# Issuing the first 25 slots of a top-k attention and MLP kernel step by step from a table

## The chip, the core and the metric

The kernel runs on one core of one Trainium2 chip. The core has a matrix engine (TensorE, PE in the profile, with its weight loads shown as PEld), a vector engine (VectorE, DVE), a scalar engine (ScalarE, ACT), a general engine (GpSimd, POOL) and an engine that only issues transfers (SyncE, SP). Each engine works through its own queue in order; between engines, an instruction waits on semaphores. The metric is the device time of one execution in microseconds.

## The reference

```python
# q, k, v: (8 batches, 8 heads, 576 positions, 64)
scores = q @ k.T / sqrt(64)                       # per batch and head, 576 x 576
kth = 32nd largest score of each row
scores = where(scores >= kth, scores, -1e9)
attn = softmax(scores)                            # sum + 1e-9 in the denominator
x = (attn @ v) -> (4608 tokens, 512)              # heads side by side
h = x @ w_in                                      # 512 -> 2048
g = h * sigmoid(1.702 * h)
out = g @ w_out                                   # 2048 -> 512
```

All data is float32.

## The kernel before, in words

**Slots.** The attention is cut into 144 slots, 18 per batch. A slot holds 128 rows of two heads. For a slot, TensorE computes the scores (`scores`, L339) into one pair of PSUM banks that all slots share; ScalarE copies them to SBUF (`copy_scores`, L350); VectorE pairs the two halves of each row by maximum and minimum (`pair_up`, L360), which frees the banks for the next scores; and VectorE then finds the 32 largest in four rounds of MAX8 and three of MATCH_REPLACE8 (`topk`, L386 and L390). GpSimd makes the threshold and the shift of the exponent from the result (`bounds`, L404 and L405). One slot later ScalarE masks (`mask`, L418) and exponentiates (`exps`, L428), which also gives the row sums `den`. `invert` adds 1e-9 (L437 on GpSimd for n > 11, L439 on VectorE up to slot 11) and takes the reciprocal on VectorE (L441).

**From probabilities to x.** Up to slot 10 the probabilities are turned on TensorE against a diagonal of the reciprocals, which GpSimd makes (`divide`, L448; `turn`, L468 and L471), and ScalarE copies the result out (L476). From slot 11 GpSimd scales them (`normalize`, L454), ScalarE splits them into halves (`split`, L490), SP writes them to DRAM (`rows<-sc`, L492) and reads them back transposed (`pt<-rows`, L498). TensorE multiplies with v (`values`, L526; `values_at`, L557; `values_of_two`, L586) and ScalarE copies the result into x.

**The MLP.** When 128 rows of x are whole they form a block. A block is worked off in four units: `hidden` (TensorE, L662), `tanh` (ScalarE, L678), `gate`, `combine` and `project` (TensorE, L760 for the first two blocks, L776 for the others). `tanh(False)` leaves the hidden values in PSUM, and then `gate` is one VectorE instruction (L693). `tanh(True)` copies them to SBUF too (L681), and then `gate` is two GpSimd instructions (L690, L691).

**The weights.** w_in and w_out come in 32 pieces, loaded by SP (L134) and rounded in steps: size (ScalarE or GpSimd), shift (VectorE, L158), low (ScalarE, L159), sign and addition (GpSimd, L148 and L151). Two or three pieces belong to each of the slots 0 to 10.

**What sets the order.** The order is written by hand and taken as it stands, with no scheduler: `opening`, then `slot(n)` for slots 0 to 10, `filling` for 11 to 20, then `steady_pair(n)` for two slots at a time from 21 on, to the last slot. Within these functions the calls issue their instructions at once; an engine's queue holds them in the order of the calls. `stay_warm` (L174) issues matmuls of the identity whose result is not used. TensorE's pieces have three tile sizes: 128x128 (the first two blocks' MLP, the turning), 128x64 (the other blocks' MLP, the values) and 64x64 (scores, ends of the values).

The lines that the change touches stand in `invert`, `slot`, `filling_slot` and at the end of the kernel:

```python
    with tc.manual_schedule():
        opening()
        for n in range(SETTLED + 1):
            slot(n)
        filling()
        for n in range(STEADY + 8, N + 2, 2):
            steady_pair(n)
```

Of the kernel before, what the change touches and what calls it, by code (L numbers as in the profile page):

```python
# [9 lines left out]
ALU = mybir.AluOpType  # L10
# [19 lines left out]
TO_ZERO = 2.0**-100  # L30


@with_exitstack
def kernel(
    ctx: ExitStack,
# [23 lines left out]

    nc = tc.nc

    B, H, S, D = q.shape
    C = H * D
# [23 lines left out]
    PAIRED = SETTLED + 1  # L89
    STEADY = PAIRED + 2  # L90
# [25 lines left out]
    both_banks = [ps_p.tile([P, 512], F32, name=f"po{i}") for i in range(2)]  # L116

    ident = const.tile([P, P], F32, name="ident")
    make_identity(nc, ident[:])
    win = const.tile([P, CC, DFF], F32, name="win")  # L120
    wout = const.tile([P, FC, C], F32, name="wout")

# [47 lines left out]
    def stay_warm(count, of=ident[:]):  # L170

        none = both_banks[1][:]
        for i in range(count):
            nc.tensor.matmul(none[:, 0:P], lhsT=of, rhs=of, start=True, stop=True)  # L174
# [147 lines left out]
    N = len(slots)  # L322
# [110 lines left out]
    def invert(n):  # L433

        some = small.tile([P, 2], F32, name="some", tag="sums")
        if n > PAIRED:
            nc.gpsimd.tensor_scalar(some[:], st[n]["den"][:], 1e-9, None, op0=ALU.add)  # L437
        else:
            nc.vector.tensor_scalar_add(some[:], st[n]["den"][:], 1e-9)  # L439
        rden = st[n]["rden"] = small.tile([P, 2], F32, name="rden", tag="inverse")  # L440
        nc.vector.reciprocal(rden[:], some[:])  # L441

# [190 lines left out]
    class Block:  # L633
        def __init__(self, place, rows):
            self.place, self.rows = place, rows
            self.whole = len(blocks_seen) < WHOLE
            self.bank = 1 - len(blocks_seen) % 2
            blocks_seen.append(self)
            self.left = list(range(FC))
            if not self.whole:  # L640
                self.left = [h * (FC // 2) + 2 * u + c for u in range(4) for h in range(2) for c in range(2)]
            self.done = 0
# [30 lines left out]
    def tanh(aside):  # L673

        if to_gate:
            ph, fs, x = to_gate.pop(0)
            th = thp.tile([P, G * P], F32, name="th")
            nc.scalar.activation(th[:], ph, AF.Tanh, scale=0.851 / RAISE)  # L678
            if aside:
                h = thp.tile([P, G * P], F32, name="h", tag="th")  # L680
                nc.scalar.copy(out=h[:], in_=ph)  # L681
                ph = h[:]
            gated.append((th, ph, fs, x, aside))
# [223 lines left out]
    def opening():  # L907

        stay_warm(8, v_tail[:, 0, :, :].rearrange("p j d -> p (j d)"))
        load("q", 0, 0, nc.sync)  # L910
        load("k", 0, 0, nc.scalar)
        for hp in range(2):
            for name in "qk":
                if hp:
                    load(name, 0, hp)
        for x in by_slot[0]:
            load_piece(x)
        prepare_first()
        scores(0)
        pair_first()  # L920
        stay_warm(2)
        for name in "qk":
            prepare_main(name, 0, 1)
        stay_warm(8)
        prepare_ends(0, 1)
        early.extend(round_piece(x) for x in by_slot[0])
        for piece in early:
            piece["size"]()
        scores(1)
        copy_scores(1)  # L930
        prepare_rest()
        for hp in range(2, NP):
            for name in "qk":
                load(name, 0, hp)
        load_v(0, 0)
        for x in by_slot[1]:
            load_piece(x)
# [11 lines left out]
    def slot(n):  # L949

        todo = later.pop(n, [])
        for fn, args in todo:
            if fn not in (prepare, prepare_by_dma, load_piece):
                fn(*args)
        preparing = [(fn, args) for fn, args in todo if fn is prepare or fn is prepare_by_dma]
        some = [round_piece(x) for x in by_slot.get(n, [])] if n else early
        steps = {name: [piece[name] for piece in some] for name in ("size", "shift", "low")}
        last = some[-1] if len(some) > 2 else None
        if last:
            steps["size"].pop()  # L960

        def do(name, count):
            for _ in range(min(count, len(steps[name]))):
                steps[name].pop(0)()

        if n == 0:
            steps["size"].clear()
            do("low", 3)
        else:
            exponentials(n - 1, bring_all if n % 4 == 1 and n > TURNS + 1 else lambda: None)  # L970
            if n == TURNS + 1:
                stay_warm(14)
                bring_all()
            copy_scores(n + 1)
            bring_all()
            if 1 < n <= TURNS:
                turn_main(n - 2)
                turn_ends(n - 2)
            if n > TURNS + 1:
                tanh(False)  # L980
            do("size", 3)
            if n == TURNS + 1:
                do("low", 3)
                tanh(False)
        for i, op in enumerate(topk(n)):
            op()
            if i == 1:
                for _ in range(min(3, len(unfinished))):
                    finish_one()
                if last and n > 2:  # L990
                    last["pool_size"]()
            if i == (9 if n < 3 else 7):
                if n > 0:
                    divide(n - 1)
                if last and n < 3:
                    last["pool_size"]()
                while unfinished:
                    finish_one()
                for fn, args in todo:
                    if fn is load_piece:  # L1000
                        fn(*args)
            if i == 9:
                pair_up(n + 1)
            if i == 12:
                do("shift", 3)
            if i == (13 if n == TURNS + 1 else 10):
                gate()
        bounds(n)
        for piece in some:
            unfinished.extend(piece["finish"][piece is last :])  # L1010
        if n < NP:
            for fn, args in preparing:
                fn(*args)
        if n >= TURNS:
            turn_main(n - 1)
            turn_ends(n - 1)
        do("low", 3)
        if last:
            last["sign"]()
        scores(n + 2)  # L1020
        if n == SETTLED:
            copy_scores(n + 2)
        if n == 0:
            return
        idle = not ready and n < TURNS
        if 1 < n <= TURNS:
            values(n - 2, put_off if n == TURNS else None)
        if n >= TURNS:
            values(n - 1, put_off)
        if n >= NP:  # L1030
            for fn, args in preparing:
                fn(*args)
        if n > PROJECTS and may_project(2):
            project(n == SETTLED)
        if idle:
            stay_warm(8)
        if n == SETTLED:
            turn_qk(1, 0)
        hidden()
# [59 lines left out]
    def filling_slot(n, beside, pool_ahead, behind, pool_behind, late=[]):  # L1099

        todo = later.pop(n, [])
        due = [(fn, args) for fn, args in todo if fn is prepare_by_dma]
        exponentials(n - 1)
        for fn in beside:
            fn()
        for fn in pool_ahead:
            fn()
        find(n, 8)
        for fn, args in todo:
            if fn is load_v:  # L1110
                fn(*args)
        scores(n + 2)
        if n == PAIRED:
            normalize(n - 1)
            split(n - 1)
            copy_scores(n + 2)
        else:
            copy_scores(n + 2)
            normalize(n - 1)
            split(n - 1)  # L1120
        write_all()
        for fn, args in todo:
            if fn not in (prepare_by_dma, load_v):
                fn(*args)
        turn_by_dma(n - 1)
        while turns:
            turns.pop(0)()
        for fn in pool_behind:
            fn()
        bounds(n)  # L1130
        for fn in behind + late:
            fn()
        for fn, args in due:
            fn(*args)
# [106 lines left out]
    def last_units():  # L1241
# [7 lines left out]
        project_one()  # L1249
        leave_all()  # L1250

    with tc.manual_schedule():
        opening()
        for n in range(SETTLED + 1):
            slot(n)
        filling()
        for n in range(STEADY + 8, N + 2, 2):
            steady_pair(n)
        combine()
        while ready or to_gate or gated or to_combine or to_project:  # L1260
            last_units()
        merge_some(len(merging), nc.vector)
        write_all()
# [30 lines left out]
```

## Time and profile before

| what | us |
| --- | --- |
| median of 3 runs (lowest to highest) | 1378.75 (1377.12 to 1379.25) |
| the profiled execution | 1379.59 |
| its span, first to last instruction | 1377.8 |
| busy in the span: PE / DVE / ACT / POOL | 1341.2 / 1286.0 / 1164.1 / 964.4 |

The span is what the profile's rows are counted in, from its start. Two neighbouring records of an engine can overlap, so the mean duration of a record is a little more than what it adds. A busy TensorE is not TensorE at its peak, since matmuls are pipelined and their ends are modelled; a float32 matmul shows as two records.

### The profile page before, as it was taken

The numbers are of one execution on the slowest core, as the hardware profiler recorded it, in microseconds if no ns is written. First come the engines' busy times: TensorE is split into PE (matmuls) and PEld (weight loads), VectorE is DVE, ScalarE is ACT, GpSimd is POOL, SyncE is SP. The second block draws the span as 40 slices with busy tenths as digits, with TensorE's granted clock in tenths as the row PEclk, the third lists the DMA queues.
The fourth block names the chain that finished last, engine by engine and source line by source line (L and its number), as shares of the span: only waits on it lengthen the run. The fifth ranks groups of instructions, "written<-read, shape, count | busy, mean of one in ns | idle before, by whom it ended". The sixth has DMA issues, their size and how long they took to land.

```text
span 1377.8 us, 54398 instructions
## 1 busy us (share of the span) xinstructions
PE 1341.2 (97%) x22560; PEld 1205.0 (87%) x22560; DVE 1286.0 (93%) x3392; ACT 1164.1 (84%) x1930; POOL 964.4 (70%) x1758
## 2 busy tenths in 40 slices
PE   7789999999999999999999999999999999999998
PEld 5676578899999999999999999999998999999998
DVE  7999998999999999999999999999999999999912
ACT  6988887998889888988898988888888998888841
POOL 3776676777777776777777777677777777777770
PEclk8999999999999999999999999999999999999999
DMA  7551568787889786977898668988888768855640
GB/s 232 155 163 62 151 159 198 179 196 196 205 210 211 178 189 173 232 193 192 192 227 208 182 174 193 210 198 191 197 211 208 195 176 183 184 142 135 151 118 17
DMA packets 527223, 246.92 MB, mean 179 GB/s; under 512 B 458880, under 2 KB 505472, under 8 KB 526976
## 3 DMA queue, kind: packets, MB, share of 16 engines
q1 hardware_dynamic: 526544, 243.16, 71.5%
q8 instruction: 177, 2.90, 0.9%
q14 instruction: 70, 0.57, 0.1%
q10 hardware_dynamic: 432, 0.30, 0.1%
HBM read 46.01 MB, written 103.42 MB: 108 GB/s over the span
## 4 chain that ended last, share of the span: by engine, by line
PE 79%; DMA 3%; ACT 1%; issue 0%; POOL 0%; SPq 0%; DVE 0%; DVEq 0%; ACTq 0%; POOLq 0%
PE ph L662 32%; PE po L776 28%; PE o L586 10%; PE s_ps L339 9%; DMA pt<-rows 2%; DMA rows<-sc 1%; ACT pr L428 0%; ACT sc L418 0%; ACT sc L490 0%; ACT sc L350 0%; ACT halves L268 0%; ACT raws L794 0%; SPq L221 0%; POOL pr L454 0%; ACT h L681 0%
## 5 line engine op out<-in xcount | busy, mean ns | idle before, releaser
L386 DVE MAX8 top<-ranked 128x8 f32<-128x288 f32 (+1 forms) x1152 | 637.6, 596 | 0.0
L662 PE MATMUL ph<-xT,win 128*64 128x128 f32 (+1 forms) x8544 | 493.8, 273 | 0.0
L662 PEld LDWEIGHTS ph<-xT,win 128*64 128x64 f32 (+1 forms) x8544 | 469.4, 137 | 27.6 <-issue 24.1
L390 DVE MATCH_REPLACE8 ranked<-top,ranked 128x288 f32<-128x288 f32 (+1 forms) x864 | 462.4, 543 | 0.0
L490 ACT COPY sc<-pr 128x2304 uint16<-128x2304 uint16 x134 | 283.4, 2115 | 90.1 <-POOL pr L454 90.0
L454 POOL TENSOR_SCALAR pr<-pr,rden 128x576 f32<-128x576 f32 x268 | 197.9, 748 | 49.2 <-DVE rden L441 47.7
L428 ACT ACTIVATE pr<-sc,low 128x576 f32<-128x576 f32 x288 | 219.9, 769 | 0.0
L418 ACT ACTIVATE sc<-sc,cut 128x576 f32<-128x576 f32 x288 | 208.6, 779 | 4.7 <-POOL cut L404 4.7
L360 DVE TENSOR_TENSOR ranked<-s_ps,sc 128x576 f32<-128x576 f32 x286 | 201.8, 747 | 3.8 <-ACT sc L350 3.8
L776 PE MATMUL po<-raws,h 128*64 128x128 f32 x2112 | 205.3, 273 | 0.0
L776 PE MATMUL po<-wout,h 128*64 128x128 f32 x2112 | 205.3, 273 | 0.0
L350 ACT COPY sc<-s_ps 128x576 f32<-128x576 f32 x286 | 168.5, 642 | 26.9 <-PE s_ps L339 14.4
L437 POOL TENSOR_SCALAR some<-den 128x2 f32<-128x2 f32 x132 | 29.3, 222 | 221.6 <-ACT pr L428 221.4
L339 PE MATMUL s_ps<-qk_t 64*64 64x288 f32 x2304 | 177.6, 421 | 5.6 <-DVE ranked L360 4.4
L691 POOL TENSOR_TENSOR th<-th,h 128x512 f32<-128x512 f32 x134 | 171.8, 1282 | 11.2
L776 PE MATMUL po<-wout,th 128*64 128x128 f32 x2176 | 165.3, 273 | 0.0
L776 PEld LDWEIGHTS po<-raws,h 128*64 128x64 f32 x2112 | 133.8, 137 | 0.0
L776 PEld LDWEIGHTS po<-wout,h 128*64 128x64 f32 x2112 | 133.7, 137 | 0.0
L776 PEld LDWEIGHTS po<-wout,th 128*64 128x64 f32 x2176 | 127.8, 137 | 0.9 <-POOL wout L739 0.4
L339 PEld LDWEIGHTS s_ps<-qk_t 64*64 64x64 f32 x2304 | 76.2, 134 | 58.1 <-issue 14.8
L586 PE MATMUL o<-pt,v_l 128*64 128x128 f32 (+1 forms) x2240 | 124.8, 265 | 0.0
L586 PEld LDWEIGHTS o<-pt,v_l 128*64 128x64 f32 x2240 | 110.3, 137 | 10.1 <-issue 9.5
(118 smaller groups left out, 1647.5 us busy)
## 6 DMA issues: line engine op xcount, KB each, us to landing
rows<-sc SPq DMA_DIRECT2D x134, 576.0 KB, 4.0
qk_rows<-halves SPq DMA_DIRECT2D x24, 576.0 KB, 5.5
out_dram<-raws SPq DMA_DIRECT2D x68, 128.0 KB, 3.7
raws<-in_moe_w_in_dram SPq DMA_DIRECT2D x16, 512.0 KB, 5.1
raws<-in_moe_w_out_dram SPq DMA_DIRECT2D x16, 512.0 KB, 3.7
qk_l<-in_q_dram SPq DMA_DIRECT2D x28, 256.0 KB, 4.4
qk_l<-in_k_dram SPq DMA_DIRECT2D x28, 256.0 KB, 4.2
v_l<-in_v_dram SPq DMA_DIRECT2D x4, 1024.0 KB, 8.8
```

Source lines behind the costliest of these rows:

```text
L339: nc.tensor.matmul(ps[rows, i, c, 0:HALF], lhsT=qT[b, hps[p]][on, cols], rhs=kT[b, hps[p]][on, FIRST[i] + c * HALF : FIRST[i] + (c + 1) * ...
L360: nc.vector.tensor_tensor(out=ranked[n][:, :, c, :], in0=a, in1=b, op=op)
L386: nc.vector.max(top[:, i, 8 * r : 8 * r + 8], of(r, i))
L390: nc.vector.match_replace(to, top[:, i, 8 * r : 8 * r + 8], of(r, i), LOWEST)
L418: nc.scalar.activation(sc[:, i, :], sc[:, i, :], AF.Prelu, bias=cut[:, i : i + 1], scale=SCALE, alpha=HUGE)
L428: nc.scalar.activation(pr[:, i * S : (i + 1) * S], sc[:, i, :], AF.Exp, bias=low[:, i : i + 1], accum_out=den[:, i : i + 1],)
L454: nc.gpsimd.tensor_scalar(pr[:, i, :], pr[:, i, :], st[n]["rden"][:, i : i + 1], 1.0, op0=ALU.mult, op1=ALU.mult)
L490: nc.scalar.copy(out=halves, in_=pr[:].bitcast(U16).rearrange("p (k h) -> p h k", h=2))
L586: nc.tensor.matmul(o[s][j * D : (j + 1) * D, cols], lhsT=lhsT, rhs=rhs, start=(s, j) not in halves[:k], stop=(s, j) not in halves[k + 1 :],)
L662: nc.tensor.matmul(ph[rows, i * P : (i + 1) * P], lhsT=win[:, c, f * P + rows.start : f * P + rows.stop], rhs=xs[:, x.place, c, :], start= ...
L691: nc.gpsimd.tensor_tensor(out=th[:], in0=th[:], in1=h, op=ALU.mult)
L776: nc.tensor.matmul(both_banks[bank][y * TAIL : (y + 1) * TAIL, to * P : (to + 1) * P], lhsT=a[:, i, :], rhs=weight(w, fs[i])[:, y, :], sta ...
```

## The change

Every engine call of `opening`, `slot`, `filling` and the pairs 21 to 24 is now collected as a step in place of being issued, 2595 steps in all. Then the steps are issued in an order that a table gives, and from slot 25 on everything is issued at once as before. The table moves steps within and between slots, on all five engines; no engine's work is taken out by it. In the built kernel the runs of one tile size on TensorE, up to the end of the table, number 92, where they were 84.

Beside the table: the addition of 1e-9 is on GpSimd for all slots (12 instructions moved from VectorE); the first six gates, those of `slot(5)` to `slot(10)`, go by `tanh(True)`, so six VectorE instructions become six copies on ScalarE and twelve instructions on GpSimd; 14 warming matmuls in slot 5 are left out; the loads of v in `filling_slot` are issued with the other loads, behind the scores. In the built order SP issues the row write that stood just behind batch 1's load of v ahead of that load.

```diff
+COLLECTED = 25
+
+ORDER = """
+8 11 0+8 9 12 10 13+5 22 18 23+2 33 25+2 19 27+5 34 32 20 38+4 35 21 36 97 37 42+4 98 46+4 99 50 54+6 100 53 51
...
+2528+2 2516+2 2530+4 2518+6 2534+2 2585+2
+"""
+
+class Engine:
+    def __init__(self, engines, engine):
+        self.engines, self.engine = engines, engine
+
+    def __getattr__(self, name):
+        do = getattr(self.engine, name)
+
+        def step(*args, **kwargs):
+            if self.engines.collected is None:
+                do(*args, **kwargs)
+            else:
+                self.engines.collected.append(lambda: do(*args, **kwargs))
+
+        return step
+
+class Engines:
+    def __init__(self, nc):
+        self.collected = None
+        for name in ("tensor", "vector", "scalar", "gpsimd", "sync"):
+            setattr(self, name, Engine(self, getattr(nc, name)))
...
-    nc = tc.nc
+    nc = Engines(tc.nc)
...
-        if n > PAIRED:
-            nc.gpsimd.tensor_scalar(some[:], st[n]["den"][:], 1e-9, None, op0=ALU.add)
-        else:
-            nc.vector.tensor_scalar_add(some[:], st[n]["den"][:], 1e-9)
+        nc.gpsimd.tensor_scalar(some[:], st[n]["den"][:], 1e-9, None, op0=ALU.add)
...
             if n == TURNS + 1:
-                stay_warm(14)
+                pass
                 bring_all()
...
             if n > TURNS + 1:
-                tanh(False)
+                tanh(True)
             do("size", 3)
             if n == TURNS + 1:
                 do("low", 3)
-                tanh(False)
+                tanh(True)
...
-        for fn, args in todo:
-            if fn is load_v:
-                fn(*args)
         scores(n + 2)
...
-            if fn not in (prepare_by_dma, load_v):
+            if fn is not prepare_by_dma:
                 fn(*args)
...
+    def issue_in_order():
+
+        steps, nc.collected = nc.collected, None
+        order = list(range(len(steps)))
+        if ORDER.split():
+            order = []
+            for part in ORDER.split():
+                first, _, count = part.partition("+")
+                order += range(int(first), int(first) + int(count or 1))
+        assert sorted(order) == list(range(len(steps)))
+        for i in order:
+            steps[i]()
...
     with tc.manual_schedule():
+        nc.collected = []
         opening()
         for n in range(SETTLED + 1):
             slot(n)
         filling()
-        for n in range(STEADY + 8, N + 2, 2):
+        for n in range(STEADY + 8, COLLECTED, 2):
+            steady_pair(n)
+        issue_in_order()
+        for n in range(COLLECTED, N + 2, 2):
             steady_pair(n)
```

More of the change, by code (lines that the diff above doesn't have):

```diff
@@ L118 @@
     ident = const.tile([P, P], F32, name="ident")
-    make_identity(nc, ident[:])
+    make_identity(tc.nc, ident[:])
     win = const.tile([P, CC, DFF], F32, name="win")
```

81 rows, old and new, of the table ORDER are left out of this document.

## The prediction

> **What bounds the kernel now.** I read the page first (busy shares, clock, chain), then the busy time by stretch, then the waits of the first 262 us, and last the order of single instructions there.
>
> ```profile
> span 1377.8 us, 54398 instructions
> PE 1341.2 (97%) x22560; PEld 1205.0 (87%) x22560; DVE 1286.0 (93%) x3392; ACT 1164.1 (84%) x1930; POOL 964.4 (70%) x1758
> ...
> PEclk8999999999999999999999999999999999999999
> ...
> PE 79%; DMA 3%; ACT 1%; issue 0%; POOL 0%; SPq 0%; DVE 0%; DVEq 0%; ACTq 0%; POOLq 0%
> ```
>
> The chain is TensorE's, but it covers only the last 84% of the span; what comes before shows in the stretches. Their columns are length, then busy time (and instructions) of PE, PEld, DVE, ACT, POOL, then clock, DMA share, GB/s.
>
> ```profile
> core 0: us, PE busy (x) PEld busy (x) DVE busy (x) ACT busy (x) POOL busy (x), PEclk, DMA share, GB/s
> ...
> 10.40:60.00 49.60, 35.97 (x288) 26.86 (x288) 48.59 (x126) 42.99 (x88) 31.34 (x39) 0.83 0.66 208
> 60.00:140.00 80.00, 72.47 (x667) 57.98 (x666) 76.19 (x196) 69.05 (x132) 55.74 (x68) 0.98 0.37 114
> 140.00:220.00 80.00, 74.26 (x923) 55.16 (x923) 77.33 (x207) 69.85 (x119) 58.82 (x90) 1.00 0.68 169
> 220.00:262.20 42.20, 40.77 (x764) 36.74 (x762) 38.12 (x100) 32.36 (x52) 28.87 (x53) 1.00 0.76 185
> 262.20:1300.00 1037.80, 1036.56 (x18550) 949.41 (x18548) 1021.63 (x2706) 921.26 (x1494) 753.57 (x1442) 1.00 0.79 191
> ```
>
> Slots 0 to 24 of VectorE's search run from 10.4 to 262.2 us. From 262.2 on TensorE is busy for 1036.56 of 1037.80 us and the chain is its own. The code of that stage and its order are unchanged, so a microsecond won or lost before 262.2 should appear whole at the end. Before 262.2 VectorE leads: it idles 251.8 − (48.59 + 76.19 + 77.33 + 38.12) = 11.6 us, TensorE 28.3 us, of which 14.7 after 60 us. So the question is how much VectorE time the first 25 slots lose or gain, and whether TensorE keeps up.
>
> **The change part by part.** First what VectorE loses in one old slot (timeline of VectorE; start, duration):
>
> ```profile
> 104.92 0.68 DVE L693 SCALAR_TENSOR_TENSOR th<-th,po 128x512 f32<-128x512 f32 x1
> ...
> 112.40 1.14 DVE L439 TENSOR_SCALAR some<-den 128x2 f32<-128x2 f32 x1 [0.59 <-ACT pr L428]
> 113.57 0.17 DVE L441 RECIPROCAL rden<-some 128x2 f32<-128x2 f32 x1
> 113.65 1.40 DVE L386 MAX8 top<-ranked 128x8 f32<-128x576 f32 x2
> ...
> 117.01 0.68 DVE L693 SCALAR_TENSOR_TENSOR th<-th,po 128x512 f32<-128x512 f32 x1
> ```
>
> The addition waits in VectorE's queue until ScalarE's exponentials are done, and the search waits behind it. The groups up to 262.2 us (count | busy, mean ns | idle before), with GpSimd's addition from the whole run:
>
> ```profile
> L691 POOL TENSOR_TENSOR th<-th,h 128x512 f32<-128x512 f32 x11 | 14.1, 1282 | 0.9
> ...
> L439 DVE TENSOR_SCALAR some<-den 128x2 f32<-128x2 f32 x12 | 7.0, 582 | 4.2 <-ACT pr L428 4.2
> L690 POOL TENSOR_SCALAR th<-th 128x512 f32<-128x512 f32 x11 | 6.8, 621 | 0.0
> ...
> L681 ACT COPY h<-ph 128x512 f32<-128x512 f32 x8 | 4.7, 592 | 0.0
> ...
> L693 DVE SCALAR_TENSOR_TENSOR th<-th,po 128x512 f32<-128x512 f32 x6 | 4.1, 676 | 0.0
> ```
>
> ```profile
> L437 POOL TENSOR_SCALAR some<-den 128x2 f32<-128x2 f32 x132 | 29.3, 222 | 221.6 <-ACT pr L428 221.4
> ```
>
> *Twelve additions (slots 0 to 11) leave VectorE:* 7.0 busy + 4.2 idle, less 0.1 us each because records overlap (113.57 + 0.17 ends after 113.65): 10.0 us off VectorE. GpSimd takes 12 × 0.222 = 2.7 us, and now it does the waiting. VectorE's reciprocal still waits for it, but in the new order it stands later among the search steps. What is queued behind the waiting addition on GpSimd are rounding pieces; GpSimd is busy 55.74 of 80 us between 60 and 140.
>
> *Six gates leave VectorE:* 4.1 less 6 × 0.1 = 3.5 us. GpSimd takes 6 × (0.621 + 1.282) = 11.4 us and ScalarE six more copies, 6 × 0.592 = 3.6 us. Kept at the old three rounding pieces a slot, GpSimd would need about 55.74/80 × 12.1 + 1.9 + 0.2 = 10.5 us in a slot of 117.01 − 104.92 = 12.1 us: not late against the old slot, but against the unloaded 8.63 of below. The new order therefore matters: VectorE's shift of the last six pieces, in slots 9 and 10 before, stands in slots 12 and 13.
>
> *DMA queue.* In the old order SP issues the 1 MB load of batch 1's v and its two tails ahead of a row write:
>
> ```profile
> 217.75 1.41 DVE L360 TENSOR_TENSOR ranked<-s_ps,sc 128x576 f32<-128x576 f32 x2
> ...
> 226.38 1.42 DVE L360 TENSOR_TENSOR ranked<-s_ps,sc 128x576 f32<-128x576 f32 x2
> ...
> 226.58 0.59 SPq L210 DMA_DIRECT2D v_l<-in_v_dram  x1
> ...
> 227.22 1.49 SPq L221 DMA_DIRECT2D v_e<-in_v_dram  x2
> ...
> 228.76 1.14 SPq L492 DMA_DIRECT2D rows<-sc  x1
> ...
> 237.00 1.18 ACT L350 COPY sc<-s_ps 128x576 f32<-128x576 f32 x2 [4.63 <-DMA rows<-sc]
> ...
> 238.22 1.42 DVE L360 TENSOR_TENSOR ranked<-s_ps,sc 128x576 f32<-128x576 f32 x2 [2.99 <-ACT sc L350]
> ...
> 241.37 0.17 DVE L441 RECIPROCAL rden<-some 128x2 f32<-128x2 f32 x1 [1.07 <-POOL some L437]
> ```
>
> The unstalled slot is 226.38 − 217.75 = 8.63 us; the next takes 11.84, and 1.07 more are lost at the reciprocal: 4.3 us, because the write shares the engines with the load. The built order of the changed kernel has this row write ahead of the load on SP. What is late next is the transposing read behind the load, which feeds TensorE two slots later; I count the 4.3 us as won.
>
> VectorE's other idle time, 11.6 − 4.2 − 2.99 − 1.07 = 3.3 us, I leave as it is. Sum on VectorE: 10.0 + 3.5 + 4.3 = 17.8 us.
>
> *TensorE.* Its price and its waits:
>
> ```profile
> 63.69 3.39 PE L174 MATMUL po<-ident 128*128 128x128 f32 x28
> 66.92 3.74 PE L662 MATMUL po<-xT,win 128*128 128x128 f32 x32
> ...
> 102.56 2.88 PE L468 MATMUL tp<-by,pr 128*128 128x128 f32 x16 [2.17 <-POOL by L448]
> ...
> 115.94 1.95 PE L468 MATMUL tp<-by,pr 128*128 128x128 f32 x16
> ...
> 600.53 0.39 PE L776 MATMUL po<-raws,th 128*64 128x128 f32 x4
> 600.75 0.39 PE L776 MATMUL po<-raws,h 128*64 128x128 f32 x4
> ...
> 601.84 3.66 PE L662 MATMUL ph<-xT,win 128*64 128x128 f32 x64
> 605.44 1.20 PE L339 MATMUL s_ps<-qk_t 64*64 64x288 f32 x16
> ```
>
> ```profile
> PE tp L468 <- POOL by L448: 7.0, 4, 3.5
> ...
> PE tp L471 <- ACT pt L476: 6.0, 5, 3.2
> ```
>
> The 14 warming matmuls of slot 5 (28 records) go: 66.92 − 63.69 = 3.2 us. Changes of tile size: four records of one size take 600.75 − 600.53 = 0.22 us, 64 would take 3.5, and with a change behind them 605.44 − 601.84 = 3.6, so a change costs about 0.1 us. In the built order the runs of one tile size up to the end of the table number 92 against 84: the table does not reduce them, and the 8 more cost 0.8 us. So after 60 us TensorE can give 14.7 + 3.2 − 0.8 = 17.1 us if it never waited, which is no more than VectorE's 17.8. The Trainium skill, page "TensorEngine Tiling (Array Packing)", section "Key Properties", says that changing the tiling mode drains TensorE. This rule speaks against this table, which has more changes; the trace agrees with the rule, at 0.1 us a change, and the sum with it is the one above.
>
> Both engines would have to run without a wait to give 17. The waits that the new order makes are not in this trace. Bounds: none, or below nothing, since the 3.3 us left on VectorE could go too (21 us won); at the other end the largest repeated loss in a row above, the addition's 0.59 + 1.14, in each of 24 slots: 41.5 us lost, 24 us slower in all. TensorE's two waits quoted, 13.0 us, now follow a scale and a copy that run in a different order. I take 4 us, about a third of these, as the row nearest to what the table touches: **14 us won**.
>
> *Clock.* After 2.17 us of idling, 16 records take 2.88 in place of 1.95 us. If the place of the removed warming matmuls fell idle so, it would cost about a microsecond on TensorE, inside the 4. The Trainium skill, page "TensorE: Matmul & The Clock Gate", section "Part 1: The HAM clock gate", puts the idle window that halves the clock at about 3.4 us; the trace shows slower matmuls after less.
>
> The profiled execution took 1379.59 us for its span of 1377.8; the median of the three runs is 1378.75, 0.84 less. 1378.75 − 14 = about **1365 us**.
>
> **The rivals.**
> - *TensorE is the bound already from slot 5.* For it: only 5.7 us idle in 80 between 140 and 220. Against: much of that busy time is matmuls that waited in the pipeline. If it keeps three quarters of its 14.7 idle us, 3.7 + 3.2 = 7 are won: 1372.
> - *Nearly all waits go.* 17.8 + 3.3 = 21: 1358. Against it: TensorE's 17.1.
> - *Slower: in-order waits on TensorE.* The table places single pieces of one group between those of another, so a piece that waits for GpSimd's scale or ScalarE's copy (1.2 to 1.75 us each, from 6.0/5 and 7.0/4) holds the next scores, and with them the next search. It decides from 17.8/24 = 0.74 us a slot; at 1.0 it costs 24 us, 6 more than is won: 1385. For it: five engines' queues have to agree over 2595 steps. Against: the old slot had such waits too.
> - *No change:* VectorE's time goes, but the first pairs of the steady stage wait for transposed rows or TensorE and hand it back: 1379.
>
> **How the numbers follow.** Forecast (1361 to 1369) 0.48; TensorE bound 0.18; nearly all waits gone 0.09; no change 0.07; slower 0.18. A measurement here can tell about 0.2%, 2.8 us, from no change. Faster 0.48 + 0.18 + 0.09 = 0.75, same 0.07, slower 0.18. The range of 1358 to 1380 leaves out most of the slower case and the far end of the best one, 0.2 in all.
>
> **What would show it.** Right: no search step on VectorE waits for exponentials; its 25th slot ends near 248; VectorE's idle time to there below 8 us; no 4.63 us wait of the score copy; the rest of the run as long as before, 1115 us from there to the end. Wrong: VectorE's pairing waiting for the score copy in most slots; TensorE's waits for scale and copy above 13 us; the clock below 1.00 around 60 to 70 us; a steady stage longer than before by what was won.

## The result, and the profile after

| | before | after |
| --- | --- | --- |
| median of 6 runs each, us (lowest to highest) | 1378.12 (1376.03 to 1379.25) | 1372.04 (1369.34 to 1374.35) |
| ratio, 95% interval | | 0.9954 (0.9939 to 0.9969) |
| the profiled execution: time, span | 1379.59, 1377.8 | 1371.88, 1370.1 |

The change makes the kernel 6 us faster. The direction was right and the time lies in the range; of the 14 us forecast less than half arrived. The head of the page of after, and its chain that ended last:

```profile
span 1370.1 us, 54342 instructions
PE 1340.9 (98%) x22532; PEld 1202.3 (88%) x22532; DVE 1274.6 (93%) x3374; ACT 1166.2 (85%) x1936; POOL 978.4 (71%) x1782
...
PEclk9899999999999999999999999999999999999999
...
PE 86%; DMA 4%; DVE 3%; ACT 3%; POOL 1%; SPq 1%; issue 1%; DVEq 0%; ACTq 0%; POOLq 0%
```

VectorE lost 11.4 us of busy time (1286.0 to 1274.6): the twelve additions and six gates. GpSimd gained 14.0. The chain is TensorE's for 86% of the span where it was 79%. Steps that the table issues all carry line L133 here, the others L131. The same stretches as before, the last one up to the end of VectorE's 25th slot (columns as in the prediction):

```profile
10.40:60.00 49.60, 38.09 (x308) 27.09 (x307) 47.88 (x127) 43.14 (x90) 32.04 (x42) 0.86 0.68 207
60.00:140.00 80.00, 78.59 (x708) 61.90 (x707) 78.17 (x209) 76.90 (x150) 66.55 (x88) 1.00 0.41 126
140.00:220.00 80.00, 75.04 (x1023) 57.21 (x1025) 77.03 (x206) 70.21 (x117) 67.86 (x101) 1.00 0.74 173
220.00:248.10 28.10, 26.93 (x510) 24.24 (x503) 27.21 (x71) 24.82 (x42) 21.43 (x43) 1.00 0.79 202
```

VectorE's 25th slot ends at 248.1 us, 14.1 earlier than before's 262.2, just the sum that was forecast; VectorE idles 237.7 − 230.30 = 7.4 us up to there. Between 10.4 and 60 us TensorE idles 11.5 us (before 13.6), then 1.4, 5.0 and 1.2 us, 7.6 where it was 14.7; the clock is 1.00 from 60 us on. But the rest of the run takes 1370.1 − 248.1 = 1122.0 us where it took 1115.6. Two stretches of each kernel show the first part of that, before's first and then after's; they run from the start to the end of VectorE's 25th slot, and from there to the end of its 30th:

```profile
0.00:262.20 262.20, 232.82 (x2708) 185.02 (x2710) 242.53 (x632) 216.76 (x393) 175.89 (x256) 0.96 0.59 162
262.20:305.50 43.30, 43.30 (x774) 39.97 (x774) 43.30 (x117) 40.22 (x66) 31.45 (x61) 1.00 0.81 187
```

```profile
0.00:248.10 248.10, 228.01 (x2606) 178.54 (x2609) 231.24 (x614) 217.85 (x399) 189.00 (x280) 0.97 0.62 168
248.10:295.40 47.30, 47.30 (x847) 43.74 (x843) 43.65 (x117) 41.92 (x66) 32.26 (x61) 1.00 0.75 188
```

In the five slots behind, VectorE has the same 117 instructions in both kernels, but TensorE has 847 records where it had 774, and is busy without a gap: 4.0 us more. Up to the 25th slot it had done 102 fewer. Of these, 28 are the records of the 14 warming matmuls, which are gone for good; 74 have only been put behind the point by which I measured (one of them falls on the edge of the next stretch). The chain of after shows them (start, duration):

```profile
245.40 1.09 PE ph L133 x20
...
248.43 1.15 PE o L133 x21
...
249.79 0.87 PE o L133 x16
250.66 2.40 PE po L133 x44
253.06 3.06 PE po L131 x56
```

TensorE works off the table's pieces until 253.06. VectorE's rows at that time have the last search steps of slot 24 and the first one from behind the table, 5.0 us earlier:

```profile
246.73 1.41 DVE L133 MAX8 top<-ranked 128x8 f32<-128x576 f32 x2
248.06 0.80 DVE L131 MAX8 top<-ranked 128x8 f32<-128x288 f32 x2
```

TensorE's first matmul from behind the table is a point at which both kernels have the same TensorE work left, 19,840 records. In before and in after it starts at

```profile
262.94 0.61 PE L776 MATMUL po<-wout,th 128*64 128x128 f32 x8
```

```profile
252.90 0.61 PE L131 MATMUL po<-wout,th 128*64 128x128 f32 x8
```

Counted on TensorE the lead is therefore 10.0 us, not 14.1.

The waits between 60 and 250 us (in total, times, longest):

```profile
POOL some L133 <- ACT pr L133: 15.5, 14, 2.4
...
DVE rden L133 <- POOL some L133: 3.9, 6, 1.4
PEld o L133 <- DMA pt<-rows: 3.7, 3, 1.3
...
ACT sc L133 <- DMA rows<-sc: 3.4, 4, 1.3
...
PE o L133 <- DMA pt<-rows: 3.1, 3, 1.1
```

GpSimd's addition waits 15.5 us for the exponentials, which is not new: in before it waited 15.9 us between 60 and 262 us, all of it from slot 12 on. New is its wait between 60 and 140 us, 6.0 us, where before's VectorE waited 3.6. VectorE's reciprocal waits 3.9 for the sum (before 3.7). The 4.63 us wait of the score copy is gone in this trace (at most 1.3), but not in every one, as the experiments show. New is also that TensorE's products with v wait for the transposed rows.

### The profile page after: what moved, and what is told of

The parts are those of the page before. It is cut to its first block, busy times and chain, and to the rows that moved or that the text cites. A ratio compares the mean times of both kernels' runs of the same rounds, so it can differ in the third digit from the quotient of the medians.

```text
span 1370.1 us, 54342 instructions
## 1 busy us (share of the span) xinstructions
PE 1340.9 (98%) x22532; PEld 1202.3 (88%) x22532; DVE 1274.6 (93%) x3374; ACT 1166.2 (85%) x1936; POOL 978.4 (71%) x1782
## 4 chain that ended last, share of the span: by engine, by line
PE 86%; DMA 4%; DVE 3%; ACT 3%; POOL 1%; SPq 1%; issue 1%; DVEq 0%; ACTq 0%; POOLq 0%
PE ph L131 31%; PE po L131 28%; PE o L131 10%; PE s_ps L131 9%; PE po L133 4%; DMA pt<-rows 2%; DVE ranked L133 2%; PE o L133 1%; DVE top L133 1%; PE s_ps L133 1%; SPq L131 1%; PE ph L133 1%; PE tp L133 1%; ACT sc L133 1%; DMA rows<-sc 1%
## 5 line engine op out<-in xcount | busy, mean ns | idle before, releaser
L131 DVE MAX8 top<-ranked 128x8 f32<-128x288 f32 (+1 forms) x952 | 526.7, 595 | 0.0
L131 PE MATMUL ph<-xT,win 128*64 128x128 f32 x8064 | 464.2, 273 | 0.0
L131 PEld LDWEIGHTS ph<-xT,win 128*64 128x64 f32 x8064 | 441.2, 137 | 25.9 <-issue 21.9
L131 DVE MATCH_REPLACE8 ranked<-top,ranked 128x288 f32<-128x288 f32 x714 | 382.0, 543 | 0.0
L131 ACT COPY sc<-pr 128x2304 uint16<-128x2304 uint16 x120 | 253.7, 2114 | 87.0 <-POOL pr L131 87.0
L131 POOL TENSOR_SCALAR pr<-pr,rden 128x576 f32<-128x576 f32 x240 | 177.3, 749 | 40.0 <-DVE rden L131 40.0
L131 PE MATMUL po<-wout,h 128*64 128x128 f32 x2000 | 194.2, 273 | 0.0
L131 PE MATMUL po<-raws,h 128*64 128x128 f32 x2000 | 194.2, 273 | 0.0
L131 ACT ACTIVATE pr<-sc,low 128x576 f32<-128x576 f32 x240 | 183.4, 770 | 0.2 <-POOL raws L131 0.2
L131 POOL TENSOR_SCALAR some<-den 128x2 f32<-128x2 f32 x120 | 26.7, 222 | 209.8 <-ACT pr L131 209.8
L131 ACT ACTIVATE sc<-sc,cut 128x576 f32<-128x576 f32 x240 | 174.1, 781 | 0.1
L131 DVE TENSOR_TENSOR ranked<-s_ps,sc 128x576 f32<-128x576 f32 x236 | 166.6, 747 | 4.3 <-ACT sc L131 4.3
L131 POOL TENSOR_TENSOR th<-th,h 128x512 f32<-128x512 f32 x123 | 157.7, 1282 | 10.3
L131 PE MATMUL po<-wout,th 128*64 128x128 f32 x2064 | 156.6, 273 | 0.0
L131 ACT COPY sc<-s_ps 128x576 f32<-128x576 f32 x234 | 138.0, 642 | 19.8 <-PE s_ps L131 9.7
L131 PE MATMUL s_ps<-qk_t 64*64 64x288 f32 x1872 | 140.5, 415 | 0.0
L131 PEld LDWEIGHTS po<-wout,h 128*64 128x64 f32 x2000 | 126.4, 137 | 0.0
L131 PEld LDWEIGHTS po<-raws,h 128*64 128x64 f32 x2000 | 126.4, 137 | 0.0
L131 PEld LDWEIGHTS po<-wout,th 128*64 128x64 f32 x2064 | 121.3, 137 | 0.0
L131 PE MATMUL o<-pt,v_l 128*64 128x128 f32 (+1 forms) x2144 | 120.7, 266 | 0.0
L131 PEld LDWEIGHTS o<-pt,v_l 128*64 128x64 f32 x2144 | 106.6, 137 | 9.9 <-issue 9.1
L131 POOL TENSOR_TENSOR h<-th 128x128 f32<-128x128 f32 x248 | 114.1, 460 | 0.3
```

Source lines behind the costliest of these rows:

```text
L131: do(*args, **kwargs)
```

## The experiments

A kernel's progress is read here at the end of the last MAX8 of a slot on VectorE: slot 24 (the 25th, the end of the table), slot 40 and slot 140. "Steady" is the time between the last two. The ratio is to the runs of before that were taken beside each kernel, so it is not exactly the quotient of two medians of the table. All times in us.

| kernel | median | ratio to before (95%) | slot 24 | slot 40 | steady |
| --- | --- | --- | --- | --- | --- |
| before, first trace | | | 262.2 | 402.3 | 884.9 |
| before, second trace (e12) | 1376.98 | 0.9997 (0.9986 to 1.0007) | 259.1 | 399.2 | 885.7 |
| after, first trace | 1372.04 | 0.9954 (0.9939 to 0.9969) | 248.1 | 392.2 | 887.3 |
| after, second (e4) | 1372.49 | 0.9949 (0.9931 to 0.9967) | 249.7 | 393.9 | 886.4 |
| after, third (e14) | 1371.56 | 0.9959 (0.9946 to 0.9972) | 247.2 | 391.1 | 885.2 |
| e1 no table | 1392.68 | 1.0106 (1.0086 to 1.0127) | 274.2 | 415.2 | 884.3 |
| e2 table to slot 11 | 1375.83 | 0.9994 (0.9984 to 1.0005) | 257.5 | 398.6 | 885.8 |
| e3 table from slot 12 | 1394.00 | 1.0126 (1.0107 to 1.0145) | 271.7 | 415.8 | 884.3 |
| e5 no table, additions back | 1381.37 | 1.0026 (1.0009 to 1.0043) | 262.1 | 403.1 | 883.4 |
| e6 no table, warming back | 1390.04 | 1.0099 (1.0084 to 1.0114) | 272.7 | 413.8 | 884.4 |
| e7 table, additions back | 1373.87 | 0.9974 (0.9963 to 0.9984) | 255.0 | 399.0 | 883.5 |
| e8 table, gates back | 1375.04 | 0.9976 (0.9962 to 0.9990) | 253.9 | 398.0 | 886.7 |
| e9 less MLP work | 1366.01 | 0.9914 (0.9899 to 0.9929) | 247.4 | 390.6 | 882.4 |
| e10 late work | 1374.51 | 0.9987 (0.9975 to 0.9999) | 253.0 | 404.0 | 883.0 |
| e11 v load first | 1373.16 | 0.9966 (0.9954 to 0.9978) | 251.9 | 395.8 | 884.8 |
| e13 late work, 4 times | 1402.35 | 1.0183 (1.0169 to 1.0197) | 248.1 | 425.3 | 882.6 |

**The table and the edits apart.** First the edits without the table, and the table for one half of its steps. In e2 and e3, k is the number of steps that are collected before slot 12.

```diff
 e1: -ORDER = """ 8 11 0+8 ... """
     +ORDER = ""
 e2: +order = [i for i in order if i < k] + list(range(k, len(steps)))
 e3: +order = list(range(k)) + [i for i in order if i >= k]
```

> All edits beside the table stay (additions and first six gates off VectorE, no warming matmuls, loads of v behind the scores), but the collected steps are issued in the order of the program. Theory (the table is what lets TensorE follow VectorE; the edits alone leave TensorE's waits of slots 0 to 11 as they were, and only the 3.2 us of warming matmuls go from its queue): about 3 us faster than before, 1375, that is 3 us slower than the changed kernel. Rival 1 (the edits are the whole gain, the table does nothing): 1372. Rival 2 (the edits without the table cost, since VectorE now waits for GpSimd's addition in every slot): 1380 or more.

> The table's order for the steps up to the issue of slot 12, program order behind them, all other edits kept. Theory (all that TensorE won, 10 us, it won by slot 11; the table's second half won time on VectorE alone, which TensorE's pace takes back in slots 25 to 29): as the changed kernel, 1372, TensorE 9 to 11 us ahead of before from slot 12 on. Rival (the second half of the table carries a good part of the gain): 1375 or more.

> Program order up to the issue of slot 12, the table's order from there. Theory: as the kernel without the table, 1375, since the second half wins nothing that lasts. Rival (the second half makes up for what the first lost, because TensorE has waits left to give there): 1372.

Without the table the edits do not win 3 us, they cost 15. So the table is worth 20 us against its own edits. The second rival of e1 held, with a larger price than it named. The waits of e1 between 60 and 250 us (its collected steps carry line L49), where after has 3.9 us in the first row:

```profile
DVE rden L49 <- POOL some L49: 24.8, 11, 2.8
...
PEld tp L49 <- POOL by L49: 11.6, 4, 4.7
POOL some L49 <- ACT pr L49: 11.2, 8, 2.9
PE tp L49 <- POOL by L49: 10.8, 4, 4.5
```

In the order of the program VectorE waits up to 2.8 us a slot for GpSimd's addition. TensorE's turning then waits for GpSimd's diagonal, which is made from the reciprocals, and the scores stand behind the turning in TensorE's queue.

The table's first half alone (e2) is 12 us ahead at slot 11 (130.5 against 142.5 us). Slot 12 then takes 19.3 us, probably since work that the table had drawn ahead no longer fits the program's order (no run isolates this), and at the end no difference from before is left. The seam makes e2 a poor test of the first half by itself. The second half alone (e3) is 2.5 us ahead of e1 at slot 24 and 0.6 behind at slot 40; its time is not better. But 1.3 of the 2.5 us stand at slot 10 already (144.9 against 146.2), where both have issued the same steps in the same order, and 2.2 at slot 11. And its slot 12, at the seam, takes 10.9 us against e1's 8.6. So e3 wins little on VectorE that could have lasted, and is no clean test of it. In the changed kernel too most is won early: at slot 11 its three traces are at 132.5, 129.7 and 130.5 us, before's two at 142.5 and 141.0, which is 10.9 us by the means.

The two halves also show where the 4.0 us behind the table come from. From the end of slot 24 to that of slot 29, e2 (program order in this half, ahead of before) and then e3 (the table's order in this half, behind before):

```profile
257.50:301.80 44.30, 44.30 (x792) 40.98 (x792) 43.61 (x117) 40.40 (x66) 31.35 (x61) 1.00 0.72 183
```

```profile
271.70:319.00 47.30, 47.30 (x847) 43.74 (x843) 43.64 (x117) 41.89 (x66) 32.22 (x61) 1.00 0.76 188
```

e3 has no lead and takes the same 47.3 us for the same 847 records as after. So the longer stretch belongs to the records that the table's second half leaves behind; the stage does not take back a lead as such. (The other edits leave some behind too: e2 has 792 records where before has 774, and takes 1.0 of the 4.0 us longer.)

**Which edit costs without the table.** The additions on VectorE again up to slot 11, or the 14 warming matmuls back:

```diff
 e5: +if n > PAIRED: nc.gpsimd.tensor_scalar(some[:], ...)
     +else: nc.vector.tensor_scalar_add(some[:], st[n]["den"][:], 1e-9)
 e6: -pass
     +stay_warm(14)
```

> The kernel without the table (1392.7, 15 us slower than before), with the additions of slots up to 11 back on VectorE. Theory (in program order the moved additions cost: VectorE's reciprocal waits 29.0 us for GpSimd's sum in 14 places, where the moved work was 10.0 us; the wait is up to 2.8 us a slot since the addition stands in GpSimd's queue behind other work): 13 to 17 us faster than without the table, 1376 to 1380. Rival (the missing 14 warming matmuls cost it, the granted clock is 0.89 between 60 and 140 us against 0.98 before): within 4 us of 1392.7.

> The kernel without the table, with the 14 warming matmuls of slot 5 back. Theory (additions cost): 1390 to 1396, and the clock between 60 and 140 us stays near 0.89, since TensorE idles 2 us in every slot while VectorE waits. Rival (clock): 1378 to 1384 with the clock at 0.98.

The additions cost 11.3 us of the 15 (1392.68 − 1381.37); the forecast was 13 to 17, so a few us belong to the other edits. Warming gives 2.6 us by the medians, inside both intervals. The stretch from 60 to 140 us of e1, and then of e6:

```profile
60.00:140.00 80.00, 65.86 (x559) 52.91 (x560) 62.71 (x159) 63.33 (x122) 61.76 (x80) 0.89 0.37 118
```

```profile
60.00:140.00 80.00, 67.01 (x607) 54.59 (x608) 63.17 (x160) 66.07 (x126) 62.28 (x80) 0.96 0.37 116
```

With the warming back the clock is 0.96, against the 0.89 I expected to stay, and VectorE is busy for the same 63 of 80 us. So the clock was not what held these slots.

**Which edit pays under the table.** The same additions back on VectorE with the table kept; then the first six gates as one VectorE instruction each, in the place of the second GpSimd step (their copies on ScalarE stay):

```diff
 e7: as e5, with the table
 e8: +if len(gates) <= 6: nc.vector.scalar_tensor_tensor(out=th[:], in0=th[:], scalar=1.0, in1=h, ...)
```

> The changed kernel with its table, but the additions of slots up to 11 on VectorE. Theory (under the table the additions on GpSimd are on time, so they are worth what they were priced at, 10.0 us on VectorE, of which at most the 4 us that the steady stage takes back anyhow and the 7 us of idle time cover a part): 3 to 10 us slower than the changed kernel, 1375 to 1382. Rival (the table alone makes the gain, the place of the additions does nothing): 1372.

> The changed kernel with its table, but the first six gates are each one instruction on VectorE (the six copies on ScalarE stay). Theory: 3.5 us more on VectorE, most of it inside the 4 us that are taken back: 0 to 3 us slower, 1372 to 1375. Rival (the moved gates are what lets TensorE run, since a gate on VectorE waits in its queue behind a search): 5 us or more slower.

By medians the additions are worth 1.4 to 2.3 us against the three medians of after, by the ratios 2 to 3.4: at or below the theory's lower end, and not nothing. The intervals of e7 and of after overlap a little, so this is only just clear of the noise. At slot 24 the trace of e7 is 6.7 us later (255.0 against the mean of 248.3), but that is not the price of the additions: 3.8 us of it are a wait for a row write between slots 22 and 24, which the changed kernel has in its second trace too (below). At the end of slot 20, ahead of that wait, e7 stands at 215.2 us. The five traces that issue after's own steps up to there (after, e4, e14, and also e10 and e13, whose edits come later) stand at 209.4 to 213.5, 211.7 in the mean: 3.5 us.

In e7 VectorE's additions wait only 0.3 us for the exponentials up to slot 24, where before's waited 4.2. So under the table this idle time goes without the move, and the move can win only the rest of its term. The six gates are worth 2.6 to 3.5 us by the medians and 2.3 to 3.7 by the ratios, near what they were priced at, and as little clear of the noise.

**What bounds the table's second half.** Half of the products of ten MLP units are left out:

```diff
+if not x.whole and nc.collected is not None and c in (1, 2):
+    nc.collected.append(lambda: None)
+    continue
```

> The changed kernel with half of the products left out in the ten MLP units (hidden, 128x64 pieces) that the table places up to slot 24; the output is not the reference's. It takes about 10 x 3.66 / 2 = 18.3 us from TensorE between 150 and 250 us and nothing from the other engines. Theory (TensorE's 7.6 idle us between 60 and 250 are waits for transfers and other engines, and 4.1 us of its work, 74 records, stand behind the end of VectorE's 25th slot where before had it ahead): only those 4.1 us and little beside are won, 4 to 7 us faster than the changed kernel, 1365 to 1368, and VectorE's 25th slot still ends near 245 to 248. Rival (TensorE's own work is the bound from slot 12 to 24): 12 us or more faster, 1360 or less, with the 25th slot ending before 238.

The stretches of this kernel from the start, over the five slots behind the table, and from 140 to 220 us:

```profile
0.00:247.40 247.40, 215.92 (x2302) 162.69 (x2304) 231.07 (x614) 217.72 (x399) 189.10 (x280) 0.97 0.62 168
247.40:293.80 46.40, 46.40 (x832) 43.07 (x832) 43.60 (x116) 41.32 (x66) 31.64 (x61) 1.00 0.85 191
...
140.00:220.00 80.00, 66.42 (x843) 46.95 (x844) 76.45 (x207) 70.61 (x117) 66.62 (x101) 0.98 0.75 178
```

Some 300 records less, 17 us by 3.66 for 64 and 12.1 us by the busy time (228.01 to 215.92), leave the end of VectorE's 25th slot where it was, 247.4 against 247.2 to 249.7. TensorE simply idles, 13.6 us of 80 where it was 5.0. So in slots 12 to 24 VectorE is the bound under the table, and the rival falls. The time came out as the theory said, 6 us lower, but not for its reason: TensorE still has 832 records in the five slots behind, so the work put behind hardly shrank. Only 1.8 of the 6 us are there at slot 40 (390.6 against a mean of 392.4); the rest is a shorter steady stage, and no run shows why it is shorter.

**Does a lead last?** Forty products of the first steady MLP unit are repeated, then 160; and both kernels are traced again.

```diff
 e10: +for _ in range(5): product(True)    # ahead of each of the unit's 8 first products
 e13: +for _ in range(20): product(True)
 e4, e14: the changed kernel; e12: the kernel before
```

> The changed kernel with 40 of the first steady MLP unit's products repeated (80 records, 4.6 us of TensorE by the 3.66 us of 64), in slot 25, with the same result. It takes 4.6 us of the lead away behind the table. Theory (TensorE bounds every slot from there on, a lead appears whole at the end): 4.6 us slower than the changed kernel, 1376.5 to 1377. Rival (the steady stage takes a part of any lead back at fixed places, as at slots 42, 43 and 54 of the first trace): 1 to 3 us slower, 1373 to 1375.

> As the run with late work, but four times as much: 160 products repeated in slot 25 (320 records, 18.3 us of TensorE by 3.66 us for 64). Theory (what TensorE loses or wins before the steady stage appears whole at the end, within the scatter of the steady stage's own waits of 882 to 887 us between slots 40 and 140): 16 to 19 us slower than the changed kernel, 1388 to 1391. Rival (the steady stage takes about half of any lead or lag back): 8 to 11 us slower, 1380 to 1383.

> The changed kernel once more, for its spread and a second trace. If the 2.3 us that the first trace loses in the steady stage at slots 42, 43 and 54 (rows written late, the transposing read behind them late) are a matter of the single execution, they stand at other slots or are absent here, and the time is 1370 to 1374. If they belong to the order, they stand at the same slots.

> The changed kernel a third time. If its steady stage is longer by nature, slots 40 to 140 take 886 to 887.5 us again, with losses above 1 us at slots 42, 54 and 114; if that was chance, they take 882 to 885.5.

> The kernel before once more, for a second trace of its steady stage. If the first trace of before lost unusually much at slots 42 and 54 (0.6 and 1.9 us over the 17.63 us of a pair), this one loses at other places or less, and then the steady stage's differences of 1 to 2 us between traces belong to the single execution. If they come back at the same slots, they belong to the program.

The stretch from the end of slot 24 to that of slot 29, in e10 and then in e13:

```profile
253.00:307.30 54.30, 54.30 (x927) 50.76 (x923) 43.70 (x117) 41.97 (x66) 32.30 (x61) 1.00 0.67 166
```

```profile
248.10:328.50 80.40, 80.40 (x1167) 76.89 (x1163) 43.66 (x117) 41.84 (x66) 32.11 (x61) 1.00 0.46 112
```

The repeats took longer than I had priced them. The stretch grew from 47.3 to 54.3 and to 80.4 us, so 80 records cost 7.0 and 320 cost 33.1 us. Of 33.1 us, 30.3 arrive (1402.35 − 1372.0): neither theory had the number, but nothing like half is taken back. Of 7.0, 2.0 to 3.0 arrive by the medians, and 4 to 5 by the ratios. What is missing in both stands in the steady stage: 882.6 and 883.0 us, where the changed kernel took 887.3, 886.4 and 885.2, and the kernel before 884.9 and 885.7.

In all sixteen traces this stage exceeds its usual 17.6 us a pair by more than 0.5 us at the same few places only, the pairs that end with slots 42, 54, 78, 90, 96, 114, 126 and 132, by up to 3.7 us and in changing amounts. The changed kernel lost 2.8, 1.2 and 2.7 us at slot 42 and 3.5, 3.4 and 3.1 at slot 54; before lost 0.7 and under 0.5 at the one and 1.9 twice at the other. One of them on ScalarE in the first trace of after:

```profile
512.49 1.18 ACT L131 COPY sc<-s_ps 128x576 f32<-128x576 f32 x2 [3.86 <-DMA rows<-sc]
```

The score copy needs the buffer that a row write still reads. So these losses belong to the program's transfers at these slots, and their size changes with the execution and the kernel. After's stage is 1.0 us longer than before's in the mean, less than the traces of one kernel differ. Why it stands at the long end of 882 to 887 is not settled.

The second trace of before also ended its 25th slot 3.1 us earlier than the first. Slot 22, where the loads of v meet the row write, ended 11.3 us after slot 21, and not 12.9.

The changed kernel has a wait of the same kind, a little later and not in every execution. Its second trace (e4):

```profile
232.34 0.64 ACT L133 COPY sc<-s_ps 128x576 f32<-128x576 f32 x1 [3.87 <-DMA rows<-sc]
...
239.43 1.42 DVE L133 TENSOR_TENSOR ranked<-s_ps,sc 128x576 f32<-128x576 f32 x2 [4.57 <-ACT sc L133]
```

The traces of e7, e8 and e10 have it too, with 3.8, 3.6 and 3.6 us lost on VectorE; those of after, e14, e3, e9 and e13, whose transfers there stand in the same order, lose at most 1.7 us to it. That is why e10 ends slot 24 at 253.0 us and e13 at 248.1, though both issue after's steps up to there. So one trace places slot 24 to within some 6 us only. What decides whether the wait comes is not known.

**The order on SyncE.** The three loads of batch 1's v stand ahead of the row write again:

```diff
-... 2046 ... 2047 ... 2048 ... 2049 ...
+... 2047+3 2046 ...
```

> The changed kernel with the three loads of batch 1's v put ahead of the row write that precedes them on SyncE, as before had them. The prediction counted 4.3 us won for this order. Theory (TensorE, not VectorE, sets the time of these slots under the table, and the transposed rows come late either way): 0 to 2 us slower than the changed kernel, and the score copy of that slot waits for the row write again. Rival (the price holds): 3 to 4.3 us slower, 1375 to 1377.

Its waits between 215 and 262 us:

```profile
ACT sc L132 <- DMA rows<-sc: 4.9, 1, 4.9
...
DVE ranked L132 <- ACT sc L132: 3.7, 1, 3.7
```

The wait is back as it was, and VectorE loses 3.7 us; against the mean of after's three traces e11 is 3.6 us later at slot 24 and 3.4 at slot 40. The runs are 0.7 to 1.6 us slower by the medians, 1.0 to 2.3 by the ratios, and the interval of e11 (0.9954 to 0.9978) overlaps all three of after, so no difference of the times is shown. The theory's 0 to 2 us agrees with that, but its reason (that TensorE sets these slots) does not show in the trace, and e9 speaks against it.

## Why the prediction was right and wrong

*The bound* was read rightly. VectorE led up to the 25th slot and TensorE from there on, and e9 shows it for slots 12 to 24 of the changed kernel too. For its slots 5 to 11 no run decides: between 60 and 140 us VectorE idles 1.8 us and TensorE 1.4.

*What VectorE would win* came out at slot 24, 14.1 us in the traces compared and 12.3 between the means of two and three traces, with the signs that were named for it: the end near 248 us, less than 8 us idle, no long wait of the score copy, the clock at 1.00. That it came out at just 14 is in part luck: terms of the sum were too large, and the second trace of after has a wait of 3.87 us of the score copy.

*The step that failed* is the premise of the first part: "a microsecond won or lost before 262.2 should appear whole at the end", with the sign that the rest would take 1115 us. It takes the end of VectorE's 25th slot for a point at which both kernels have done the same. They have not: the changed kernel leaves 74 more records of TensorE behind it. The stage behind is TensorE's, so these cost 4.0 us there (43.3 to 47.3 us for the next five slots). At the point where TensorE has the same work left the lead is 10.0 us (262.94 and 252.90), and it is 10.1 at slot 40. e3, which takes the same 47.3 us without a lead, shows that these records cost the time. I had compared the orders for how often the tile size changes, and not for how much of each engine's work stands ahead of that point.

*The account.* By the means of the traces VectorE is 12.3 us ahead at slot 24 and 8.4 at slot 40, so the work left behind took 3.9 us. At slot 140 it is 7.3, with 1.0 us in the steady stage's row writes. The medians of the three comparisons give 6.1, 4.5 and 5.8 us. Most of the 12.3, 10.9, stands at slot 11 already. The other 1.8 of the 14.1 are scatter: the prediction was built on a trace of before whose opening was slow, and was compared with a trace of after without the wait for the row write. With e10 and e13, which issue the same steps up to there, after's mean at slot 24 is 249.2 and the lead 11.4. The last 1 to 2 us between traces and runs are within their spread of 5 us.

*The terms of the sum.* "Twelve additions leave VectorE" at 10.0 us was the one most mis-sized. The reciprocal still needs the sum, so the addition only changes who waits for the exponentials; by itself the move costs 11.3 us (e1 against e5) and under the table it gains 1.4 to 3.4. Of the 4.2 us of waiting that the term counted, all but 0.3 go without the move (e7). The text said that the reciprocal "stands later among the search steps" in the new order. It should have said that the whole term depends on it. The gates at 3.5 held (e8: 2.6 to 3.5). The 4.3 us of the v load were a price from one execution; the second trace lost 11.3 − 8.63 = 2.7 us there, after's second trace lost 4.57 with the new order, and by the times nothing clear of the noise is shown for the order (e11: 0.7 to 2.3). The warming matmuls, at 3.2 us, gave 2.6 the other way in e6, and TensorE's busy time up to the point of equal work fell by only 0.7 us (233.7 to 233.0); which other records grew is not shown. The price of the 8 more changes of tile size was not tried by itself.

*TensorE's waits.* I left TensorE 17.1 − 14 = 3.1 us of waits after 60 us; it kept 7.6. Of the 5.0 between 140 and 220, 3.1 are new waits for transposed rows, while VectorE is the bound there (e9 makes these waits 8.3 us, and the slots no later).

*The rivals.* "TensorE is the bound already from slot 5" named the time, 1372, and not the mechanism: e9 refutes it for slots 12 to 24, and for slots 5 to 11 it was not tested. "Slower by in-order waits" did not come under the table, but e1 shows how near it was: the same edits in the old order gave 1393, through VectorE's wait for GpSimd rather than TensorE's for its pieces.

## What to carry to other kernels

Before a lead is carried from one stage into the next, count what every engine still has to do at the point where it is read, or read it at a point where the next bound engine has the same work left. A search step that ends 14 us earlier is worth only 10 if the next bound engine has been left 4 us more work. Moving an instruction off the bound engine pays only if its result is there when the bound engine needs it: the same twelve additions cost 11 us in one order and gained some 2 in the other. And a stall seen in one execution should be looked up in a second before it is entered as a price, and its absence in one execution before it is entered as a gain.

## What the runs showed of the hardware that I had not expected

Repeating one 128x64 product on the same 64 columns took 33.1/320 = 0.103 us a record, where the unit's normal order, which alternates between the two halves of the columns, takes 3.66/64 = 0.057. Record by record, e13's repeats start 0.109 us apart; where the halves alternate, records start 0.055 us apart, in two interleaved rows with 0.109 us from one to the next. So the two halves run beside each other, and the order within one tile size matters as well. The Trainium skill, page "TensorEngine Tiling (Array Packing)", section "Key Properties", says that different tiles can load weights and multiply in parallel; these runs agree, and they price what is lost when neighbours in the queue share a tile: 0.046 us a record.
